# Attention and token mixing on one core: a tile's values in one transfer, and a new table of the order of all work

## The chip, the cores and the metric

The kernel runs on one core of a Trainium2 chip. The core has five instruction streams that matter here: TensorE (PE: matrix products; its weight loads, PEld, overlap them), VectorE (DVE), ScalarE (ACT), GpSimd (POOL) and SyncE (SP, which issues every transfer of this kernel). The metric is the device time of one execution in microseconds (us); lower is better. The text gives medians over several executions, and the profile is one further execution.

## The reference

Two stages follow each other on a batch of 4 sequences of 768 positions (8 heads of 64, so 512 columns); everything is float32.

```python
# attention: each position sees the positions less than 16 away, and 24 block summaries
k_sum = k.reshape(B, H, nb, 32, D).max(axis=3)
v_sum = v.reshape(B, H, nb, 32, D).mean(axis=3)
scores_l = where(|i - j| < 16, scale * q @ k.T, -1e9)
scores_s = scale * q @ k_sum.T + log(32)
a = softmax(concat(scores_l, scores_s))
x = a @ concat(v, v_sum)                       # [4, 768, 512]
# mixing
theta = x @ w_theta
zr, zi = x * cos(theta), x * sin(theta)
y = w_tok_r @ zr + w_tok_i @ zi                # over the 768 positions
u = x + y
out = u + maximum(u @ w_ch, 0)
```

## The kernel before

The work is written as a list of small operations, each with its engine or a choice of engines. A table of numbers, `ORDER`, names every operation once, in the order in which all of them are issued; a letter behind a number picks the engine (g GpSimd, d VectorE, a ScalarE). Each engine takes its own operations in that order, strictly one behind the other, and waits on semaphores for what an operation needs. So the table alone decides what stands ahead of what on each engine. One rule is added at issue: a GpSimd operation that shares the memory port with VectorE waits for the VectorE operation that precedes it in the table.

Attention works in 24 tiles (4 batches of 6) of 128 positions, each in two halves of 64 queries. For a tile (`att_tile`) SP loads q (`q<-qg`, 256 KB, two buffers), the values (`v<-vg`) and, for batches 1 to 3, the keys. TensorE forms the scores (line 523), VectorE subtracts the maximum (559), ScalarE takes the exponential (563), TensorE turns the result (572), ScalarE or VectorE copies it out (578), and TensorE multiplies it with the values (`products`, 546). The values of a half are 96 rows of 2,080 bytes (8 heads of 64 numbers and a one, which sums the weights), 195 KB; 24 rows of block summaries are copied in ahead of them. There are four value buffers, so a tile's values can only land once the products of two tiles before have ended.

Then the tile is turned back (605), and the theta product follows: for the first 6 tiles in plain float32 (639), later as three products of split numbers (644), four groups each into one bank `t`. Rounding, sine and cosine follow (655 to 668, on ScalarE and VectorE), and the product with x (674, half on VectorE, half on GpSimd) gives the input of the token mixing. Batches 0 and 1 are mixed directly (702, `mix_step`, the products M), tile by tile. Batches 2 and 3 use a scheme with seven products MP1 to MP7 (817, `mix_fast`). Each MP has 12 pieces of three matrix products (6 tiles, two column halves). MP6, MP7, MP5 and MP3 take summed weights, streamed by SP from `s_scratch` into the second halves of six `wt` buffers (384 KB each); a buffer is loaded anew when the last piece that reads it has ended. At the end the channel product with `w_ch` (922) and the relu follow, and SP writes the output.

At most 8 transfers are under way: each one waits for the end of the one issued eight before.

Of the kernel before, what the change touches and what calls it, by code (L numbers as in the profile page):

```python
# [29 lines left out]
NK = NB + NL  # L30
VL = 96
# [27 lines left out]
253 104 85 98 215 214 110 223 216 296g 258 224 99d 225 243 255 257 217 118 348g 226 105 227 218 119g 220d 293 256 245 219d 106
244 246 228 247 250 111 120 221 291 121 249 222d 248 123 124g 297 229 122 349g 298 345 259 230 260 262 292 299 261 270 130 125  # L60
301 350g 115 300 271 263 126 272 303 423g 305 302 304 306 273 267d 308 131g 307 116 264d 419 310 135 268 309 265 274 313 127
136g 132 311 312 266d 141 275 269d 314 276 133 315 142g 137 317 316 277 138 352 143 112 231 325 326 318 232 134 327 163 233g
139 144 353 361 168 319d 356 328 320 329 362 278 330 322 355 234 169g 145 331 346 164g 321d 279 364 323 363 282 117 146 324
283 420 332 354 113 347 284 280 365 474 285 147 380 358 114 357 339 165 360 148 366 359 337 166 367 338 149 167 170 368 150
152 381 424 369 422 333 370 400 153 382 128 383 384 171 334 154 172 155 157 281 158g 156 425 385 371 402 401 159 372 386 340
174 335 175g 373 426 392 394 374 421 160 375 377 376 378 387 529 161 404 176 388 379 403 705g 389 454 177 530 179 395 393 178
180 455 456 390g 472 408 457 181 405 182 410 183 427 703 458 459 414 466 409 412 460 461 462 463 411 435 428 467 429 704g 406
437 706g 438 415 431 430 441 468 615g 469 413 436 434 464g 707 521 442 433 465 432 416 417 407 479g 440 564d 523 443 439 480
288g 741 709g 534 444 446d 418 481 535 482 445 485 483 447 490 477 129 492 491 484 475 448 478g 493 486 496 449 451d 532 710g
452 743 450d 488 531g 522 453d 497 616g 487 536 509 537 539 494 586 476d 540 489 538 495 498 510 621 499 391g 501 543 500d 541  # L70
742 511 502 512 545 503 506 513 542 547 551 504 546 733 507 583 289g 286g 708g 549 505d 550 533g 343g 548 544 745 508d 514 744
552 553 515 341 554 555 524 516 556d 517 711 712 518 287g 713d 714 739 585 336g 557 344g 398 734 587 596 558d 599 519 624 588
603 559 715 592 589 716 746 717 561 668 568 591 562 565g 622 735 593 718 566 719 584 560d 597 140 601 720 595 563 598 567 600
602 399g 784 590 594 623 342 569 785d 604 473g 721 786 740 605 572 625 607d 570 634 606 576 608 626 635 787g 617 788 653g 722
618 665 638 151 789 629 574 697 637 630 396d 397g 470 619 525g 723g 737 639 627 790 698g 609d 620 636 628 520 832 612 633 736
471g 162 641 833g 654g 659g 613 738 834g 631 791 640 610 611d 632 792 614d 655 841 642 747 752 643 835g 669 526 644d 793 645
670 646 812 678 672 657 679 650 813d 671 173 667 683 681 658 814d 815 680 663 647d 836 673 748 842 816 675 664 684 843g 817
656 648 818 755 754 724 945g 837 674 682 844 819 660g 677 661 649d 651 666 527d 652 676 685 820 686 687 794 839 689 821 688d
795 838g 756 1015 757 690 528g 571 845g 975 765 662 822 759 760 976d 850 691 840 977d 578 846 978 851g 796 768 823 727d 763
184 797 852 946 699 766 758 692 853g 769 1020 701 694d 979 940 702 980 700 941 847g 772 848 693d 579 981 825 767 695 749 696d  # L80
761 762 771 731 753 750 764 580g 798d 824 982 728 770 732 773 983 774 775d 984 947 956 581g 776 854g 777 995 948 729 778d 959
849 781d 949 950 958 725g 582g 802 952 803 996 997 998 953 799g 859 751 943 1016 1021 779 951 782 855 999 730 780 1074 1000
985 860g 1001 856 800 726 963 1018 808 857 1002 942 954 861g 957 961 960 962 801 955 575 826g 783 964 862 863g 1077 858 944g
965 1003 1022 966 1004 986 967d 864g 968 1005 806 804 1017g 810 1031 972 868 805 865g 1050 828 1023 1051d 1052 1032 869g 573
577 987 829 1170 1053 830 1024 866 1025 1033 989g 1006 969d 1054 827 1035 1037 831 1029 1055 870 1028 993 871 1056 1007g 970
872g 1027 1034 867 973 1120d 1038 1008 877 994 1036 1026 1057 1019d 1058 1013 1030 971 1014 974d 873d 1059 1039 874g 1040 1042
1078 878 1041d 809 811 990g 1079 1043 1047d 1208 1076 807 1087 1089 991 876 992 1209 1088 1090 1011 1210d 1083 1094 1093 1044d
1060 879 1009 880 1211 1080 1212 875 881 1082 1129 1012 1045 882g 1048 1213 886 1061 1126 1081 1092 1066 883 1075 1010 884
1084 1091 1214 1063g 1085 887 1067 885 1062 1127 1121 1046d 988 888 1215 1086 1173 1068 1049 1216 895 1095 1096 1098 1106g
1130 1217 1097d 889 1099 1218d 1279 1107g 1280 1281g 1069 1131 1070 896 1071 1228 1133 1100d 1282 1064g 1219 1135 890 1103d  # L90
1229 1283 1072 1073 1139 1065 891g 1137 1132 1110 1141 892 1142 1101 1284 1111 897 1143 1104 1285 1134 1138 1102d 898g 1108
1105d 1145 899g 1146 1286 1140 1144 1136 1109 1287 1128 893 900d 1158d 1147 1148 901g 1150 894 1288 1172 1250 1149d 1118 1174
1289 1114 1175 1112 1151 1305 1116 1178 1179 902 1202 1236 1122 1152 1183 903 1221g 1123 1306 1124 1185 1307 1308g 1187 1177
1181 1309 1153 904 1182 1160 1184 1232 1310 1155 1189 1237 1230 1233 1220g 1188 1176 1125 1186 1311 905 1156 1162 1171 1290
1312 906g 1249 1154 1163 1203 1247 1190 1180 1157 1234 1313 1159g 1191 1192 1193 1291g 1231 1251 1314 1222g 1194d 907 1315d
1252 1254 1195 1235 1292g 1117 1354 1240 1196 1253 1355 1260 1261 1356 1161 1199d 1255 1357g 1166 1168 1319 1197 1358 1198d
1322 1256 1257 1241 1258 1164d 1165g 1169 908g 1316 1263 1242 1200 913 1359 1206 1264 1360 1259 1207 1201d 1243 909 1324 1361
# [1025 lines left out]
```

## Time and profile before

| | |
|---|---|
| time, median of 3 runs | 435.1 us (434.0 to 435.14) |
| profiled execution, span from the first to the last instruction | 435.6 us |
| TensorE busy | 421.7 us, 97% |
| VectorE busy | 352.2 us, 81% |
| ScalarE busy | 280.3 us, 64% |
| GpSimd busy | 209.7 us, 48% |
| transfers: share of 16 DMA engines' time on the queue | 71.1% |

The profiled execution's span is 0.5 us longer than the median of the runs. The busy shares are means over the span; the start, the mixing of the first tiles and the end have limits of their own.

### The profile page before, as it was taken

To read this page: it belongs to the slowest core of one execution; us is meant where nothing else is said; L and a number is where in the kernel's file an instruction comes from. 1 tells how busy PE (TensorE), PEld (TensorE's weight loads), DVE (VectorE), ACT (ScalarE), POOL (GpSimd) and SP (SyncE) were. 2 spreads that over 40 slices of the span, in tenths; PEclk is the share of its full clock that TensorE was granted. 3 is DMA by queue.
4 is the path that set the end of the run, shared out by engine and by line. 5 is a ranking of instruction groups with operands and counts; after the bars stand their busy time and mean duration, and the time that the engine had idled before them with its cause. 6 is when DMAs were issued, how large, how long until landed. Compare 5 with 4: busy or idle time off the path is not lost.

```text
span 435.6 us, 10044 instructions
## 1 busy us (share of the span) xinstructions
PE 421.7 (97%) x3682; PEld 350.9 (81%) x3682; DVE 352.2 (81%) x947; ACT 280.3 (64%) x600; POOL 209.7 (48%) x208
## 2 busy tenths in 40 slices
PE   5989999998999999999999999999999989999996
PEld 1455555665888888888888899999899989999996
DVE  3799999778988777875757695866489989999996
ACT  1799995787757784866785885493955447455210
POOL 3543324687775665245465578624453410251542
PEclk9899999999999999999999999999999999999999
DMA  8999956989678678848767987883379696220138
GB/s 294 347 354 364 295 197 208 290 257 322 230 233 273 197 224 266 259 139 247 232 188 223 292 273 218 245 246 119 111 230 338 229 367 223 75 73 20 65 136 289
DMA packets 76321, 100.07 MB, mean 230 GB/s; under 512 B 23024, under 2 KB 58864, under 8 KB 76272
## 3 DMA queue, kind: packets, MB, share of 16 engines
q1 hardware_dynamic: 76272, 99.43, 71.1%
q8 instruction: 29, 0.48, 0.5%
q14 instruction: 20, 0.16, 0.1%
HBM read 75.82 MB, written 23.59 MB: 228 GB/s over the span
## 4 chain that ended last, share of the span: by engine, by line
PE 87%; DMA 10%; DVE 1%; ACT 1%; SPq 0%; issue 0%; POOL 0%; DVEq 0%
PE m L702 25%; PE m L817 19%; PE t L644 11%; PE c L922 7%; PE m L922 6%; PE pa L546 5%; PE s L523 4%; PE t L639 3%; PE t L605 3%; DMA q<-qg 3%; PE pa L572 3%; DMA wth<-wth 2%; DMA wt<-wti 2%; DMA zu<-kT 2%; DMA wt<-s_scratch 1%; PE t L922 1%
## 5 line engine op out<-in xcount | busy, mean ns | idle before, releaser
L817 PE MATMUL m<-wt,hl 128*128 128x384 f32 x504 | 95.7, 339 | 1.4 <-DMA wt<-s_scratch 1.2
L817 PEld LDWEIGHTS m<-wt,hl 128*128 128x128 f32 x504 | 87.7, 188 | 4.9 <-ACT hl L309 1.5
L702 PE MATMUL m<-wt,hl 128*128 128x512 f32 (+1 forms) x432 | 84.9, 341 | 0.0
L702 PEld LDWEIGHTS m<-wt,hl 128*128 128x128 f32 x432 | 68.6, 188 | 10.8
L563 ACT ACTIVATE e<-e,st 128x118 f32<-128x118 f32 x192 | 63.1, 388 | 12.1 <-DVE st L559 11.6
L559 DVE CUSTOM_DVE_ANT_0 e<-s,cs 128x118 f32<-128x118 f32 x192 | 46.8, 272 | 9.6 <-PE s L523 4.7
L318 POOL TENSOR_TENSOR hl<-zu,hl 128x512 fp32r<-128x512 f32 x23 | 30.1, 1309 | 43.9 <-DMA wt<-s_scratch 15.9
L644 PE MATMUL t<-wth,xh 128*128 128x512 f32 x144 | 45.3, 396 | 0.0
L674 POOL TENSOR_TENSOR zu<-xn,zu 128x512 f32<-128x512 f32 x20 | 27.0, 1350 | 20.3 <-ACT zu L668 5.5
L657 DVE SCALAR_TENSOR_TENSOR zu<-zu,t 128x512 f32<-128x512 f32 x24 | 16.4, 684 | 24.4 <-ACT zu L655 24.4
L702 PE MATMUL m<-wt,zu 128*128 128x512 f32 (+1 forms) x96 | 33.4, 491 | 1.2 <-DVE zu L674 1.2
L655 ACT ACTIVATE zu<-t,bmagic 128x512 f32<-128x512 f32 x24 | 16.5, 687 | 23.9 <-PE t L644 18.3
L309 ACT CAST hl<-zu 128x512 fp32r<-128x512 f32 x31 | 19.1, 619 | 18.2 <-PE m L817 14.9
L702 PEld LDWEIGHTS m<-wt,zu 128*128 128x128 f32 x96 | 17.5, 190 | 15.8 <-issue 12.6
L546 PEld LDWEIGHTS pa<-v,e 118*64 118x64 f32 x768 | 24.8, 137 | 6.8 <-issue 3.0
L318 DVE TENSOR_TENSOR hl<-zu,hl 128x512 fp32r<-128x512 f32 x37 | 27.6, 751 | 2.3 <-ACT hl L309 2.1
L523 PE MATMUL s<-k,q 64*64 64x118 f32 x768 | 25.6, 272 | 3.9 <-POOL cs L340 3.2
L546 PE MATMUL pa<-v,e 118*64 118x65 f32 x768 | 28.1, 224 | 1.2 <-ACT e L578 1.2
L730 POOL TENSOR_TENSOR zu<-zu 128x512 f32<-128x512 f32 x15 | 21.4, 1432 | 15.0 <-DVE zu L730 4.9
L644 PE MATMUL t<-wth,xl 128*128 128x512 f32 x72 | 28.6, 397 | 0.0
L674 DVE TENSOR_TENSOR zu<-xn,zu 128x512 f32<-128x512 f32 x28 | 24.7, 884 | 4.8 <-ACT zu L668 4.6
L523 PEld LDWEIGHTS s<-k,q 64*64 64x64 f32 x768 | 20.2, 135 | 9.2 <-POOL cs L343 4.0
(181 smaller groups left out, 909.9 us busy)
## 6 DMA issues: line engine op xcount, KB each, us to landing
wt<-s_scratch SPq DMA_DIRECT2D x48, 384.0 KB, 4.4
v<-vg SPq DMA_DIRECT2D x48, 195.0 KB, 5.3
s_scratch<-f SPq DMA_DIRECT2D x24, 384.0 KB, 3.9
k<-kg SPq DMA_DIRECT2D x18, 376.0 KB, 5.5
q<-qg SPq DMA_DIRECT2D x24, 256.0 KB, 6.0
wt<-wtr SPq DMA_DIRECT2D x6, 768.0 KB, 11.0
wt<-wti SPq DMA_DIRECT2D x6, 768.0 KB, 11.4
f<-kT SPq DMA_DIRECT2D x12, 384.0 KB, 4.3
```

What stands on the lines that cost most here:

```text
L309: nc.scalar.copy(dst(), src())
L318: lambda e: V[e].tensor_tensor(dst(), src(), hi().bitcast(F32), op=ALU.subtract), reads, writes, due, port=BOTH)
L523: mm(0.79 * len(pairs) / NP, [lambda p=p, g=g, h=h: nc.tensor.matmul(sc[h].get()[ROW[g], p], q.get()[ROW[h], p, ROW[g]], k.get()[ROW[h], p ...
L546: mm(2 * 0.433 + scores[0] + (0.2 if scores[0] else 0.0), [lambda n=n, g=g, a=a: nc.tensor.matmul(xa[a].get()[ROW[g], n], turned[g].get()[ ...
L559: op({"DVE": 0.205}, lambda eng, n=n: nc.vector.tensor_tensor_reduce(e()[:, n], sc[n % 2].get()[:, 2 * a + n // 2], mask(m), -SCALE, 3.0e3 ...
L563: op({"ACT": 0.288}, lambda eng, n=n: nc.scalar.activation(e()[:, n], e()[:, n], AF.Exp, bias=st.get()[:, n:n + 1], scale=-1.0), [(st, n)] ...
L644: calls = [lambda t=t, xx=xx, k=k, c=c: nc.tensor.matmul(th.get(), xx.get()[:, c], w_th[c].get()[:, k], start=(c == 0 and t == 0), stop=(c ...
L674: op({"DVE": c_dve(DM, "two"), "POOL": c_pool(DM)}, lambda e, z=z, hc=hc: V[e].tensor_tensor(z(), xn[b, i].get().rearrange("p h d -> p (h ...
L702: nc.tensor.matmul(acc[th](), zz, w[:, TT[th]], start=(s == 0 and r == 0 and t == 0 and (th == 0 or c == 0)), stop=(s == NT - 1 and r == 1 ...
L730: lambda e: V[e].tensor_tensor(dst(), x(), y(), op=ALU.add if sign > 0 else ALU.subtract), reads, writes, due, port=BOTH)
L817: calls = [lambda ref=ref, tt=tt, z=z, s=s, j=j, t=t, x=x, k=k, bank=bank, first=first: nc.tensor.matmul(bank[j].get()[:, :HT], z.get()[:, ...
L922: calls = [lambda k=k, t=t, x=x, y=y: nc.tensor.matmul(to.get(), weights[n][x][0]()[:, k, j * P:(j + 1) * P], operands[n].get()[:, y, k], ...
```

## The change

Two things change. First, a tile's values come in one transfer of 96 rows of 4,160 bytes (390 KB) in place of two of 195 KB. The two halves lie side by side in one buffer, and there are two such buffers in place of four smaller ones; the bytes are the same, the number of value transfers falls from 48 to 24. Second, the whole table `ORDER` is another one. By the two tables TensorE has 548 operations before and after, VectorE 755 and 731, ScalarE 497 and 508, GpSimd 204 and 217, SP 288 and 264 (the 24 transfers). What is computed is unchanged. In the changed kernel most line numbers are lower by one.

```diff
 ORDER = """
--17g 8 0g 1g 31 23 27 25 9 24 18 29 10 28 2 26 39 3 19 32 30 20 4 44g 33 5 6g 190g 49g 46 45 48 7 50 86 194g 47 193 51 60 61 34
...
+23 8 25 27 13 9 17g 24 26 15 39 31 43g 29 33 18 85 35 28 19 78 184 40 92 20 45 99 44 47 185 21 49 14 10 32 48 0g 1g 2 3 4 30
...
-            A1=13, T1=10, PREP=5, QB=2, VSPE=1, VB=4, KB=2, STR=2, ...
+            A1=13, T1=10, PREP=5, QB=2, VSPE=1, VB=2, KB=2, STR=2, ...
...
-            vbuf[b] = [Ref(apool, [NB + VL, H, DV], tag="v", bufs=K["VB"]) for _ in range(K["VB"])]
+            vbuf[b] = [Ref(apool, [NB + VL, 2, H, DV], tag="v", bufs=K["VB"]) for _ in range(K["VB"])]
...
-        v = [vbuf[b][(2 * i + g) % K["VB"]] for g in range(2)]
+        v = vbuf[b][i % K["VB"]]
+        dma(lambda: v.get()[NB:], lambda: vg[b, i], 2 * H * (VL + 16) * DV * 4, [], [(v, "loc")], due, 4160, 0.35)
         for g in range(2):
-            dma(lambda g=g: v[g].get()[NB:], lambda g=g: vg[b, 2 * i + g], H * (VL + 16) * DV * 4, [], [(v[g], "loc")], due, 2080, 0.35)
-            if 2 * i + g < K["VB"]:
+            if i < K["VB"]:
                 op({"POOL": ...}, lambda e, g=g: (
-                    nc.scalar.copy if e == "ACT" else V[e].tensor_copy)(v[g].get()[:NB], vs.get()), [vs], [(v[g], "sum")], due, port=BOTH)
+                    nc.scalar.copy if e == "ACT" else V[e].tensor_copy)(v.get()[:NB, g], vs.get()), [vs], [(v, ("sum", g))], due, port=BOTH)
...
-            xa[a].get()[ROW[g], n], turned[g].get()[...], v[g].get()[:NK, NH * a + n], start=True, stop=True)
-            for a in range(2) for n in range(NH) for g in range(2)] + scores[1], v + turned + scores[2], xa + scores[3], due, mode="block")
+            xa[a].get()[ROW[g], n], turned[g].get()[...], v.get()[:NK, g, NH * a + n], start=True, stop=True)
+            for a in range(2) for n in range(NH) for g in range(2)] + scores[1], [v] + turned + scores[2], xa + scores[3], due, mode="block")
```

Three places of the new order follow. The first is SP's queue in the first 40 us. Before, from the third q to the fifth (the fifth q is the one ahead of the last `v` row shown), it reads:

```order
L303 DMA q<-qg 128x512
L303 DMA v<-vg 96x520 x2
L303 DMA wt<-wtr 128x1536
L303 DMA wt<-wti 128x1536
L303 DMA q<-qg 128x512
L303 DMA wt<-wtr 128x1536
L303 DMA v<-vg 96x520 x2
L303 DMA wt<-wti 128x1536
L303 DMA wt<-wtr 128x1536
L303 DMA v<-vg 96x520
L303 DMA q<-qg 128x512
L303 DMA v<-vg 96x520
```

In the changed kernel SP's queue reads, from the second tile's values to the fourth tile's:

```order
L302 DMA v<-vg 96x1040
L302 DMA q<-qg 128x512
L302 DMA wt<-wtr 128x1536
L302 DMA wt<-wti 128x1536
L302 DMA q<-qg 128x512
L302 DMA wt<-wtr 128x1536
L302 DMA v<-vg 96x1040
L302 DMA wt<-wti 128x1536
L302 DMA wt<-wtr 128x1536
L302 DMA q<-qg 128x512
L302 DMA v<-vg 96x1040
```

The fifth q now stands ahead of all of the fourth tile's values, where one half of them preceded it before. It is the 28th transfer before and the 24th after, and the bytes ahead of it fall by that half.

The second place is TensorE at tile 5's first mixing product (`m<-wt,zu`, the first row of that form below; `t<-wth` are the four groups of tile 6's theta product, each of two rows). Before:

```order
L644 MATMUL t<-wth_926,xh 128x512 x2
L644 MATMUL t<-wth_926,xl 128x512
L644 MATMUL t<-wth_887,xh 128x512 x2
L644 MATMUL t<-wth_887,xl 128x512
L644 MATMUL t<-wth_972,xh 128x512 x2
L644 MATMUL t<-wth_972,xl 128x512
L702 MATMUL m_722<-wt,zu 128x512
L702 MATMUL m_704<-wt,zu 128x256
L644 MATMUL t<-wth_1011,xh 128x512 x2
L644 MATMUL t<-wth_1011,xl 128x512
L702 MATMUL m_702<-wt,zu 128x512
L702 MATMUL m_704<-wt,zu 128x256
```

After, the same place on TensorE:

```order
L643 MATMUL t<-wth_689,xh 128x512 x2
L643 MATMUL t<-wth_689,xl 128x512
L643 MATMUL t<-wth_739,xh 128x512 x2
L643 MATMUL t<-wth_739,xl 128x512
L643 MATMUL t<-wth_954,xh 128x512 x2
L643 MATMUL t<-wth_954,xl 128x512
L643 MATMUL t<-wth_912,xh 128x512 x2
L643 MATMUL t<-wth_912,xl 128x512
L701 MATMUL m_718<-wt,zu 128x512
L701 MATMUL m_683<-wt,zu 128x256
L701 MATMUL m_681<-wt,zu 128x512
L701 MATMUL m_683<-wt,zu 128x256
```

The fourth theta group has moved ahead of the first mixing product of tile 5.

The third place is TensorE where batch 3 goes from MP6 to MP7. The number behind `wt` is the weight buffer, that behind `hl` the operand. Before, the last eight pieces of MP6 and the first four of MP7 (the buffers of MP7 in their order: 1206, 1235, 1495, 1498, 1507, 1832):

```order
L817 MATMUL m2_4508<-wt_1495,hl_4579 128x384 x3
L817 MATMUL m0_4556<-wt_1495,hl_4579 128x384 x3
L817 MATMUL m0_4556<-wt_1498,hl_4579 128x384 x3
L817 MATMUL m2_4508<-wt_1498,hl_4579 128x384 x3
L817 MATMUL m2_4508<-wt_1507,hl_4601 128x384 x3
L817 MATMUL m2_4508<-wt_1832,hl_4601 128x384 x3
L817 MATMUL m0_4556<-wt_1507,hl_4601 128x384 x3
L817 MATMUL m0_4556<-wt_1832,hl_4601 128x384 x3
L817 MATMUL m2_4508<-wt_1206,hl_4629 128x384 x3
L817 MATMUL m2_4508<-wt_1235,hl_4629 128x384 x3
L817 MATMUL m0_4556<-wt_1206,hl_4629 128x384 x3
L817 MATMUL m0_4556<-wt_1235,hl_4629 128x384 x3
```

After, the same stretch (the buffers of MP7 in their order: 1012, 1193, 1154, 1553, 1462, 1887):

```order
L816 MATMUL m0_4549<-wt_1154,hl_4582 128x384 x3
L816 MATMUL m0_4549<-wt_1553,hl_4582 128x384 x3
L816 MATMUL m2_4467<-wt_1154,hl_4582 128x384 x3
L816 MATMUL m2_4467<-wt_1553,hl_4582 128x384 x3
L816 MATMUL m2_4467<-wt_1462,hl_4568 128x384 x3
L816 MATMUL m0_4549<-wt_1462,hl_4568 128x384 x3
L816 MATMUL m0_4549<-wt_1887,hl_4568 128x384 x3
L816 MATMUL m2_4467<-wt_1887,hl_4568 128x384 x3
L816 MATMUL m0_4549<-wt_1012,hl_4590 128x384 x3
L816 MATMUL m0_4549<-wt_1193,hl_4590 128x384 x3
L816 MATMUL m0_4549<-wt_1154,hl_4608 128x384 x3
L816 MATMUL m2_4467<-wt_1012,hl_4590 128x384 x3
```

The fifth buffer (1507 before, 1462 after) is now free one piece earlier, and the third (1495 before, 1154 after) is needed earlier: seven pieces lie between the end of its use in MP6 and its first use in MP7, where ten did.

## Rows read from the trace of the kernel before

**Rows 1.** The page, busy time by engine: us, share of span, instructions.

```profile
PE 421.7 (97%) x3682; PEld 350.9 (81%) x3682; DVE 352.2 (81%) x947; ACT 280.3 (64%) x600; POOL 209.7 (48%) x208
```

**Rows 2.** Waits of TensorE: line, releaser, us in total, times, longest.

```profile
PE s L523 <- POOL cs L340: 3.2, 1, 3.2
PE t L379 <- POOL zu L377: 1.4, 1, 1.4
PE m L702 <- DVE zu L674: 1.2, 1, 1.2
PE pa L546 <- ACT e L578: 1.2, 2, 0.7
PE m L817 <- DMA wt<-s_scratch: 1.2, 1, 1.2
PE s L523 <- DMA q<-qg: 0.4, 1, 0.4
PE m L817 <- DVE x L826: 0.2, 1, 0.2
```

**Rows 3.** Windows: us, busy PE, PEld, DVE, ACT, POOL, PEclk, DMA share, GB/s.

```profile
11.00:45.00 34.00, 31.36 (x399) 18.11 (x400) 30.83 (x127) 30.44 (x73) 15.57 (x27) 0.95 1.04 354
364.00:432.00 68.00, 67.81 (x388) 67.32 (x387) 66.57 (x107) 25.47 (x43) 24.12 (x14) 1.00 0.35 121
```

**Rows 4.** Critical chain from 20 to 46 us: start, us, what.

```profile
18.58 9.06 DMA wt<-wti
...
27.66 11.64 DMA q<-qg
...
39.44 1.04 PE s L523 x32
```

**Rows 5.** Windows in which value rows move (first) and don't (second).

```profile
28.00:31.00 3.00, 3.00 (x26) 1.28 (x29) 3.00 (x14) 3.00 (x9) 1.17 (x2) 1.00 1.05 300
24.00:28.00 4.00, 3.34 (x55) 2.48 (x52) 3.96 (x16) 4.00 (x11) 1.32 (x3) 1.00 1.01 405
```

**Rows 6.** Critical chain from 90 to 103 us.

```profile
89.73 2.15 PE t L639 x5
...
97.62 2.31 DVE zu L674
...
99.98 1.56 PE m L702 x4
101.54 0.70 PE t L644 x3
```

**Rows 7.** GpSimd's timeline beside it: start, us, engine, line, operation.

```profile
97.55 1.83 POOL L318 TENSOR_TENSOR wt<-wt 128x768 fp32r<-128x768 f32 x1
```

**Rows 8.** Line 674 on VectorE: duration in ns, min/median/max.

```profile
L674 DVE TENSOR_TENSOR zu<-xn,zu x28: 659/685/2303, 45.1 to 330.5; 128x512 f32<-128x512 f32 x28
```

**Rows 9.** Critical chain from 335 to 360 us.

```profile
345.49 5.85 DMA wt<-s_scratch
...
353.31 0.57 DVE x L826
```

**Rows 10.** TensorE's timeline, pieces of MP1 to MP7 back to back.

```profile
326.02 24.26 PE L817 MATMUL m<-wt,hl 128*128 128x384 f32 x138
```

**Rows 11.** Transfer issued at 341.33, first for MP7: us from issue to landing.

```profile
wt<-s_scratch SPq DMA_DIRECT2D x1, 384.0 KB, 3.5
```

**Rows 12.** Transfer issued at 342.89, third for MP7.

```profile
wt<-s_scratch SPq DMA_DIRECT2D x1, 384.0 KB, 4.6
```

**Rows 13.** Transfer issued at 346.10, sixth for MP7.

```profile
wt<-s_scratch SPq DMA_DIRECT2D x1, 384.0 KB, 6.2
```

**Rows 14.** Transfer issued at 351.36, behind twelve others of that burst.

```profile
wt<-s_scratch SPq DMA_DIRECT2D x1, 384.0 KB, 9.2
```

**Rows 15.** Window of MP7's first load (columns as in rows 3).

```profile
341.00:343.00 2.00, 2.00 (x13) 2.00 (x12) 2.00 (x5) 1.15 (x3) 0.00 (x0) 1.00 0.17 17
```

**Rows 16.** The wait for bank t, from TensorE's timeline.

```profile
32.81 0.66 PE L605 MATMUL t<-cs,xn 128*128 128x128 f32 x4 [0.68 <-DVE zu L657]
```

More of the change, by code (lines that the diff above doesn't have):

```diff
@@ L59 @@
[L59 to L62, printed above, removed]
@@ new lines @@
+180 469 403 400 387 285 429 450 698 451 452 181 453 454 182 404 693g 455 405 695g 406 462 432 463 388 460 522 456 431 457
+458g 286g 421 424 423 409 428 696d 410 425 407 408 556 401 430 461 514 427 435 433 411 434 412 422 426 436 699g 516 437 438
+402 472g 439 440d 283 526 413g 339g 332g 473 474 475 471g 477 476 481 441 527 478 442 483 443 515 445 722 482 479 446 724
+444d 447d 480 284g 502 486 485 487 730 484 488 150 490 723 470g 489 491 725 386g 503 575 577 528 492 494 523 493d 697g 524
+391g 529 504 495 531 535 496 497 537 539 466g 530 541 538 533 337g 525g 532 731 505 506 507 459g 540 499d 536 542 498d 534
@@ new lines @@
+1589 1677 1449 1454 1456 1555 1590g 1666 1669 1672 1667 1670 1680 1594 1675 1673 1556 1683 1475 1439 1514 1515 1516g 1436
+1518 1458 1455 1597d 1448 1450 1452 1437 1557 1702 1438d 1440 1598g 1459 1676 1679 1443 1678 1681 1684 1682 1685 1457 1604g
+1711 1447 1453 1451 1474 1558 1686 1460 1717 1461 1441 1462 1463 1476 1559d 1464d 1600g 1465 1466 1611g 1742 1477 1470 1687
+1689 1688 1601d 1479 1467 1602 1478 1481 1468 1608g 1743 1690 1692 1471 1694 1519 1480 1485 1744g 1691 1606d 1607g 1693 1695
+1696 1697 1560 1745 1699 1616 1746 1747 1517g 1612d 1482 1748 1486 1484 1469d 1472 1613 1489 1749 1483 1490 1487 1491 1520
@@ new lines @@
+1731 1734 1723 1726 1729 1732 1799 1737 1721 1724 1727 1766 1767 1769g 1546 1547 1778 1814g 1768 1815g 1779 1780d 1548 1886
+1784 1730 1889 1785 1786 1806 1787 1733 1736 1739 1735 1738 1898 1895 1807 1800d 1788 1789 1790 1791 1781 1801 1826 1741 1855
+1804g 1805g 1857 1783 1859 1740 1792 1869 1793 1856 1858 1871 1782 1860 1862 1827 1861 1873 1875 1823 1794 1795 1796 1802
+1883 1797 1803 1864 1863 1865 1808d 1809 1877 1892 1867 1866 1822g 1977 1978 1812 1818 1879 1819 1990 1870 1813 1979 1996
+1872 1874 1868 1997 1831 1998g 1820 1876 1991 1878 2020 2022 1840 1881 1816g 1880 1882 1830 1992g 1824 2021 1817 1843 1884
@@ new lines @@
+2050 2064d 2066 2095 2067 2053 2166 2054 2093 2057 2060 2154 2164 2098 2073 2070 2061 2074 2155 2077 2078 2071 2108 2081
+2096g 2187 2111 2217 2209 2075 2079 2102 2058 2218 2132 2128 2134 2107 2113 2100 2112 2082 2076 2109 2224 2150g 2103 2129
+2120 2151 2110 2121 2116 2130 2105g 2114 2156 2133 2117 2141 2152 2131 2135 2137 2142 2153g 2124 2138 2118 2139 2188 2167
+2143 2226 2161 2171 2145 2122 2157 2192 2159 2160g 2072 2125 2115 2162 2158g 2146 2247 2083 2189 2190 2168 2173 2194 2165
+2163 2210 2193 2169 2211g 2191 2136 2170d 2172 2055 2197 2201 2212 2198 2199 2213g 2200 2176 2180 2221 2205 2177 2195 2248
@@ L141 @@
+2219 2080 2126 2174 2175 2184 2202 2144 2178 2220g 2214 2196 2254 2185 2206 2215 2228 2255 2059 2227d 2181 2147 2229 2216
+2222g 2249 2233 2140 2119 2186 2230 2234 2203 2062 2250 2182 2236 2235 2256 2252 2251 2253 2051 2223 2231 2179 2232d 2183
+2237 2257 2258 2261 2225g 2207 2259 2260 2123 2240 2262 2238 2204 2239 2241 2242 2244 2245 2243 2246 2263 2264 2265 2266 2267
 """
@@ L546, in products @@
         mm(2 * 0.433 + scores[0] + (0.2 if scores[0] else 0.0), [lambda n=n, g=g, a=a: nc.tensor.matmul(
-            xa[a].get()[ROW[g], n], turned[g].get()[:NK, (NH * a + n) * QT:(NH * a + n + 1) * QT], v[g].get()[:NK, NH * a + n], start=True, stop=True)
-            for a in range(2) for n in range(NH) for g in range(2)] + scores[1], v + turned + scores[2], xa + scores[3], due, mode="block")
+            xa[a].get()[ROW[g], n], turned[g].get()[:NK, (NH * a + n) * QT:(NH * a + n + 1) * QT], v.get()[:NK, g, NH * a + n], start=True, stop=True)
+            for a in range(2) for n in range(NH) for g in range(2)] + scores[1], [v] + turned + scores[2], xa + scores[3], due, mode="block")
         for a in range(2):
```

147 lines of the change are left out of this document (63 added, 84 removed).

## The prediction

> **What bounds the kernel now.** I read the page first: TensorE is busy 97% of the span, VectorE 81%, GpSimd under half [rows 1]. The matrix products are the same before and after, so TensorE's idle time is all that a new order can win: 435.6 - 421.7 = 13.9 us, of which its waits make some 9.5 us [rows 2]; the remaining 4 us, the first loads and the output after the last product, can't be had. The second view is TensorE's list of waits, which says where the rest lies [rows 2]: 4.6 us in two waits of the first 11 us, 2.3 us in the start-up of attention (the copies of line 578, bank t at line 605, the fifth q) [rows 2, 16], and two single holes of 1.2 us, one at the first mixing product of tile 5, one in the streamed weights of batch 3. Everything else is 0.2 us. The third view, the windows, tells two stages apart [rows 3]: from 11 to 45 us the DMA engines are full (share 1.04, 354 GB/s) while TensorE has 2.6 us of idle time; from 364 to 432 us TensorE is busy 67.81 of 68 us with VectorE at 66.57. The last stage has nothing to win, the middle one the two holes. The chain that ended last shows what the start waits for [rows 4]: not a value transfer and not an engine, but a weight transfer of 9.06 us, whose end lets SP issue the fifth q, which takes 11.64 us to land; TensorE starts on it at once.
>
> **The change, part by part.** All sums are made against the profile's 435.6 us, 0.5 us above the median of 435.1.
>
> The merged values by themselves. No wait of TensorE or of the chain names the values [rows 2, 4]. A product needed both halves before and needs them now; a buffer comes free after the same product. SP issues 24 transfers fewer, but nothing in the chain waits for SP's own issuing time. I put 0 on it directly. It has one indirect effect, on the start: while rows of 2,080 bytes move, the queue carries 300 GB/s, otherwise 405 [rows 5]. By the time the fifth q is needed three tiles' values (3 x 390 KB = 1.17 MB) have moved; at 300 GB/s that is 3.9 us, at 405 it is 2.9. The new rows of 4,160 bytes may get any part of this, 0 to 1.0 us; I take 0.4, since the first window is a mix of values and weights, so that the values alone are slower than its mean, and doubling the row will not make them as fast as rows of 6 KB.
>
> The fifth q. It is TensorE's release at 39.44. In the new order one half of the fourth tile's values (195 KB) no longer moves ahead of it, the rest ahead is the same bytes: 195 KB / 354 GB/s = 0.55 us [rows 3]. With the 0.4 us above q lands about 0.95 us sooner. To profit, TensorE must be there sooner: it came 0.44 us early before [rows 2], and the new order takes the copy of the first tile out from behind an operation that waits for a transfer, and issues the first keys ahead of the block values; the waits at line 578 (1.2 us) are what this can shorten. I take **-0.9 us**, from -0.3 (only the half transfer, q sharing the full queue) to -1.5. After 39.44 TensorE has no further wait for a transfer until 350, so this shift is kept.
>
> Tile 5's first mixing product. The hole: tile 5's theta ends at 89.73 + 2.15 = 91.88, its product with x at 97.62 + 2.31 = 99.93, 8.05 us later; TensorE goes on at 99.98, 8.1 us after 91.88, and 1.2 us of this is the wait, so that its other work covers 6.9 us [rows 2, 6]. The new order puts the fourth theta group (0.70, rows 6) ahead too: 7.6 us of cover. What makes the chain long is VectorE's operation at 97.62: 2.31 us, where the median of its kind is 0.685 [rows 6, 8]. It started 0.07 us after a GpSimd subtraction of 1.83 us and ended 0.55 us after that one's end [rows 7], as if it had run only then. In the new order that GpSimd subtraction (another weight piece by then) stands just ahead of the product with x on VectorE, and no longer behind a product with x of another tile on GpSimd, so that it can start sooner and overlap only in part. If the block goes, the chain is 8.05 - 1.62 = 6.4 us, below 7.6: the hole goes altogether, -1.2. If it stays whole, 8.05 - 7.6 = 0.5 us remain, so -0.7. I take **-1.1**.
>
> The Trainium skill, page "SBUF — State Buffer", section "SBUF: two separate sides", has a rule for this: VectorE with two SBUF inputs and GpSimd reading SBUF share one port pair as an exclusive lock, and whichever starts second waits for the whole other instruction. The 2.31 us beside the GpSimd operation's 1.83 agree with it. By the rule alone, with GpSimd's subtraction starting first again, the term is -0.7; by the row's median it is -1.2.
>
> MP7 of batch 3. A piece takes 24.26/46 = 0.527 us [rows 10]. Before, nine pieces (4.74 us) lie between the release of the fifth buffer and its next use; its load took 5.85 us [rows 9], so TensorE waited 5.85 - 4.74 = 1.1, shown as 1.2 [rows 2]. Now ten pieces (5.27 us) lie there, for the first, fourth and sixth too, nine for the second, but seven (3.69 us) for the third. The third load took 4.6 us [rows 12]; it would be late by 0.9, or by 0 if it lands as the first did, in 3.5 [rows 11]; I take 0.4. The sixth took 6.2 us [rows 13] against 5.27 plus those 0.4: 0.5 late. So 0.8 to 0.9 us of waiting in place of 1.2: **-0.3 us**, between -1.2 (all land in time) and +1.0 (the third takes 5.85: 2.2 late).
>
> Banks. Between two MP groups VectorE adds the bank to the output (0.57 us, rows 9) before the next group may write to it. One piece of 0.52 us covered it once before, and cost 0.2 us [rows 2]; by the new order one piece must do three times (MP1 to MP6, MP6 to MP7, MP7 to MP4), one of them swallowed by the weights' wait: **+0.3**, 0 to +0.6.
>
> New tight places. Between a theta product and the next user of bank t, by the order and the products' durations, TensorE has 1.57 us of other work at the tiles X1 and X2 and 1.64 at X20; one of the three waited, 0.68 us [rows 16]. By the new order X1 and X2 keep 1.57, X10 and X22 have 1.65, X20 is relieved. One more such place at a third of 0.68 is +0.2; I double it for places of other kinds (the turned weights straight ahead of the first value product, scores of tile 1 with 2.7 us before their turn where there were 4.7): **+0.4**, 0 to +1.5.
>
> VectorE in the last stage loses some 3 us of work to ScalarE and GpSimd there, but TensorE waited 0.19 us of 68 [rows 3]: 0. If VectorE's cover of 1.4 us is misplaced by a new local order, that could cost the same 1.4; I leave it in the range.
>
> Sum: -0.9 - 1.1 - 0.3 + 0.3 + 0.4 = -1.6 us: 434.0 for a profile, 435.1 - 1.6 = **433.5** for the median. The likeliest case's own range is 432 to 434.3.
>
> **The rivals.** (a) *The gains go back; no change.* At the start the queue is full whatever its order, and with eight transfers under way a value transfer of 390 KB in place of 195 takes a larger share of it: if two of the eight ahead of q are such, 390 KB more at 354 GB/s are 1.1 us, and q lands 0.55 us later instead of earlier. Then +0.5 stands for -0.9, and -1.1 - 0.3 + 0.3 + 0.4 with it gives -0.2: 434.9. For it: the 11.64 us of the q, more than its own bytes need by ten times, say that it shares [rows 4]. Against: the bytes ahead are fewer. It takes in the case that the merging does nothing and VectorE stays blocked: -0.55 - 0.7 - 0.3 + 0.3 + 0.4 = -0.9, 434.2.
>
> (b) *Slower: the third streamed weight.* With 3.69 us of cover the third buffer of MP7 is the most exposed place of the new order. On an empty queue loads land in 3.5 to 4.6 us, on a loaded one in up to 9.2 [rows 11, 12, 14]. Seven other transfers (channel weights, the stored u) are issued just ahead; before, the queue was nearly empty (share 0.17) when MP7's first load was issued [rows 15]. They hang on the last theta product of the program, which the new order puts about 1 us later; if they still move, the load takes as long as in the burst: 9.2 - 3.69 = 5.5 us late in place of 1.2. With the other terms, -0.9 - 1.1 + 0.3 + 0.4 + 4.3 = +3.0: 438.1. It decides above a landing of 7.5 us: there the term is +2.6 and the total +1.3, the edge of what can be measured. Against: 1 us later leaves a part of the 2 us of empty queue.
>
> (c) *The holes go and nothing new comes*: -0.9 - 1.2 - 1.2 = -3.3, 431.8. Against: the order is tight everywhere; each wait that it has comes from a coincidence of two engines, and a new order draws these again.
>
> **How the numbers follow.** About 1.3 us (0.3%) is what can be told from no change here; faster means under 433.8, slower over 436.4. The forecast (a gain of 0.8 to 3) has 0.5, (c) 0.1, (a) 0.22, (b) and other new waits of its kind together 0.18. Of the forecast's half a quarter lies within 0.3%, since its centre is only 0.3 us beyond the edge. So: faster 0.47 (0.37 of the forecast, 0.1 of (c)), same 0.35, slower 0.18. The range reaches from (c) with a margin, 431.2, to 436.4, and leaves out the upper part of (b).
>
> **What would show it.** The fifth scores product at 38.3 to 39.0 instead of 39.44, with q still the last wait or none: right. The first mixing product of tile 5 without a wait, the VectorE product with x near 0.7 us: right; at 2.3 us again with half a microsecond of wait: it stayed blocked. At MP7 of batch 3 a wait under 1 us at the third or sixth buffer: right; several us at the third: (b). Values in the chain or in TensorE's waits, or a TensorE idle of several us in the stage after 364, would make the whole account wrong.

## The result: slower by 1.0%

The changed kernel takes 439.6 us (median of 6 runs, 437.7 to 441.4), the kernel before beside it 435.1 (6 runs, 434.0 to 435.7): a ratio of 1.0102, with a 95% interval from 1.0075 to 1.0129. The forecast was 433.5, the range 431.2 to 436.4.

First a correction to the base of the sum. In each run of both kernels the time is some 1.75 us longer than the span. The profile of before (span 435.6) thus belongs to an execution of about 437.4 us, and not to one that is half a microsecond off the median. A second profile of the same kernel (before_again, below) has a span of 433.6 and a time of 435.3. It is the better base, and stands for before from here on.

The page of the changed kernel, busy time by engine (as in [rows 1]):

```profile
PE 424.0 (97%) x3682; PEld 351.3 (80%) x3682; DVE 348.4 (79%) x923; ACT 291.9 (67%) x627; POOL 214.4 (49%) x221
```

TensorE's waits in the changed kernel (as in [rows 2]), the ones that matter here:

```profile
PE s L522 <- DMA q<-qg: 2.1, 2, 1.4
PE t L378 <- POOL zu L376: 1.8, 1, 1.8
PE pa L545 <- ACT e L577: 1.7, 3, 0.9
PE pa L571 <- ACT e L562: 1.5, 1, 1.5
...
PE m L816 <- DMA wt<-s_scratch: 0.5, 1, 0.5
...
PE m L816 <- issue: 0.3, 1, 0.3
...
PE m L701 <- POOL zu L673: 0.3, 1, 0.3
PE m L816 <- DVE x L825: 0.2, 1, 0.2
```

The wait of 1.2 us at tile 5 is gone, that of the streamed weights is under 1 us. New are two waits in the start: 1.4 us for the second tile's q (the longer of the two in the first row), and 1.5 us for ScalarE's exponentials of tile 1, which is the second tile. Windows of the changed kernel (columns as in rows 3):

```profile
11.00:45.00 34.00, 29.47 (x378) 17.66 (x379) 28.67 (x115) 29.64 (x72) 12.56 (x22) 0.95 1.03 320
20.00:24.00 4.00, 2.44 (x36) 1.54 (x36) 2.32 (x17) 3.24 (x11) 2.27 (x4) 1.00 1.02 258
36.00:40.00 4.00, 4.00 (x23) 1.75 (x20) 4.00 (x17) 4.00 (x13) 2.71 (x2) 1.00 1.06 230
23.80:27.50 3.70, 3.67 (x52) 2.72 (x52) 3.17 (x6) 3.70 (x9) 0.36 (x2) 0.71 1.01 405
```

The queue is as full as before (share 1.03) but carries 320 GB/s where it carried 354 [rows 3]; 230 to 258 while values move. The last row shows TensorE's clock behind the idle time of 1.48 us: 0.71, a mixture of its two levels (2.4 and 1.2 GHz). TensorE's timeline there, and at the scores product that had waited for the fifth q:

```profile
23.76 1.30 PE L571 MATMUL pa<-cs,e 64*118 64x64 f32 x16 [1.48 <-ACT e L562]
24.99 0.83 PE L604 MATMUL t<-cs,xn 128*128 128x128 f32 x4
25.76 1.85 PE L522 MATMUL s<-k,q 64*64 64x118 f32 x32
...
40.39 1.04 PE L522 MATMUL s<-k,q 64*64 64x118 f32 x32
...
47.11 1.13 PE L701 MATMUL m<-wt,zu 128*128 128x512 f32 x2
```

At half the clock 32 scores products take 1.85 us, else 1.04. The scores product starts at 40.39, against 39.44 [rows 4] and 38.47 in the second profile. It no longer waits there, but q has landed only just before: issued at 27.70, it took

```profile
q<-qg SPq DMA_DIRECT2D x1, 256.0 KB, 12.6
```

so it landed at 40.3, against 39.30 [rows 4] and 38.3 in the second profile.

Where the 4.9 us between the two spans arise is seen if TensorE's start of a product is set against the sum of the median durations of the products before it. That difference is its lateness. Worked out from the traces (us), after so many us of work:

```
work done            36     63     84    320    end
before_again       16.1   16.8   19.4   23.2   24.6
changed kernel     18.5   21.3   22.9   27.5   29.6
v_one              17.7   19.4   22.5   29.0   29.7
v_late             17.0   17.6   20.3   24.1   26.7
swap2              17.3   19.7   20.8   25.3   27.0
one_warm           18.4   19.9   20.9   25.4   27.1
z5_late            16.4   17.0   18.2   21.7   22.6
```

36 us of work lies behind the start of the first mixing product (44.70 us in before_again, 47.11 in the changed kernel: 2.4 us apart there too), 84 behind tile 5's, 320 ahead of the waits in MP7. The changed kernel loses 2.4 us up to the first mixing product, another 2.1 by 63, wins 1.0 back at tile 5, loses 0.8 in the 236 us that follow, and 0.7 in MP7 and behind. Each row is one execution. The two executions of before lie 1.0 us apart at the first mixing product (45.65 and 44.70) and 2.0 at the end, and v_late's took 2.1 us more than the median of its kernel; so a single difference under some 2 us in this table shows a place, and is no proof of a cost.

The 2.1 us hang on a chain that begins in the start. The chain of the changed kernel in the window from 46 us on, thinned out:

```profile
34.22 17.42 DMA wt<-wti
...
51.73 0.91 ACT f L400
...
53.14 0.95 DVE f L408
...
58.27 4.31 DMA f<-kT
...
75.97 2.51 POOL wth L317 x2
...
79.36 1.31 POOL zu L673
...
80.72 1.56 PE m L701 x4
```

A raw weight lands at 51.64; its conversion to float32 on ScalarE and VectorE, and the transfers and engines that wait for it, are then the chain for 29 us. In the second profile of before the chain from 40 to 84 us consists of TensorE's own products and nothing else. That the late start is the whole cause isn't shown: swap2 (below) starts its mixing 1.2 us sooner than the changed kernel and still loses 1.7 us against before_again in this stretch (17.3 to 19.7, against 16.1 to 16.8).

At the streamed weights the chain that ended last reads (as in [rows 9]):

```profile
346.37 4.53 DMA wt<-s_scratch
...
356.01 0.57 DVE x L825
```

It is the load of the third buffer, the third of MP7's six, and took 4.5 us; before, the chain went through the fifth buffer's, which took 5.85.

### The profile page after: what moved, and what is told of

Same layout as the page of the kernel before. It is cut to its first block, busy times and chain, and to the rows that moved or that the text cites. A ratio compares the mean times of both kernels' runs of the same rounds, so it can differ in the third digit from the quotient of the medians.

```text
span 438.5 us, 10014 instructions
## 1 busy us (share of the span) xinstructions
PE 424.0 (97%) x3682; PEld 351.3 (80%) x3682; DVE 348.4 (79%) x923; ACT 291.9 (67%) x627; POOL 214.4 (49%) x221
## 4 chain that ended last, share of the span: by engine, by line
PE 77%; DMA 14%; DVE 5%; ACT 2%; issue 1%; POOL 1%; SPq 0%; ACTq 0%; DVEq 0%; POOLq 0%
PE m L701 20%; PE m L816 18%; PE t L643 11%; PE c L921 6%; PE m L921 5%; PE pa L545 5%; PE s L522 4%; DMA wt<-wti 4%; DMA v<-vg 3%; PE pa L571 3%; PE t L604 2%; DMA q<-qg 2%; DMA f<-kT 2%; DMA zu<-kT 1%; DVE wt L411 1%; DMA wt<-s_scratch 1%
## 5 line engine op out<-in xcount | busy, mean ns | idle before, releaser
L816 PE MATMUL m<-wt,hl 128*128 128x384 f32 x504 | 92.9, 339 | 1.1 <-DMA wt<-s_scratch 0.5
L816 PEld LDWEIGHTS m<-wt,hl 128*128 128x128 f32 x504 | 87.1, 188 | 3.5 <-issue 2.3
L701 PE MATMUL m<-wt,hl 128*128 128x512 f32 (+1 forms) x432 | 80.5, 340 | 0.0
L701 PEld LDWEIGHTS m<-wt,hl 128*128 128x128 f32 x432 | 67.0, 188 | 10.0
L317 POOL TENSOR_TENSOR hl<-zu,hl 128x512 fp32r<-128x512 f32 x28 | 38.4, 1374 | 47.3 <-DVE cb L729 8.2
L308 ACT CAST hl<-zu 128x512 fp32r<-128x512 f32 x34 | 21.0, 620 | 29.2 <-PE m L816 18.4
L673 POOL TENSOR_TENSOR zu<-xn,zu 128x512 f32<-128x512 f32 x23 | 30.8, 1341 | 15.6 <-ACT zu L667 13.9
L643 PEld LDWEIGHTS t<-wth,xh 128*128 128x128 f32 x144 | 25.5, 188 | 5.1
L729 POOL TENSOR_TENSOR f<-f 128x192 f32<-128x192 f32 x35 | 21.6, 620 | 14.6 <-DVE st L588 5.1
L577 ACT COPY e<-pa 118x512 f32<-118x512 f32 x32 | 18.2, 590 | 11.5 <-PE pa L571 11.5
L317 DVE TENSOR_TENSOR hl<-zu,hl 128x512 fp32r<-128x512 f32 x32 | 23.7, 742 | 1.9 <-POOL hl L310 1.7
```

Source lines behind the costliest of these rows:

```text
L308: nc.scalar.copy(dst(), src())
L317: lambda e: V[e].tensor_tensor(dst(), src(), hi().bitcast(F32), op=ALU.subtract), reads, writes, due, port=BOTH)
L643: calls = [lambda t=t, xx=xx, k=k, c=c: nc.tensor.matmul(th.get(), xx.get()[:, c], w_th[c].get()[:, k], start=(c == 0 and t == 0), stop=(c ...
L673: op({"DVE": c_dve(DM, "two"), "POOL": c_pool(DM)}, lambda e, z=z, hc=hc: V[e].tensor_tensor(z(), xn[b, i].get().rearrange("p h d -> p (h ...
L701: nc.tensor.matmul(acc[th](), zz, w[:, TT[th]], start=(s == 0 and r == 0 and t == 0 and (th == 0 or c == 0)), stop=(s == NT - 1 and r == 1 ...
L729: lambda e: V[e].tensor_tensor(dst(), x(), y(), op=ALU.add if sign > 0 else ALU.subtract), reads, writes, due, port=BOTH)
```

## The experiments

The first four runs cross the kernel before with the changed one. Each run is timed against the kernel before on its own chip; the numbers are the median in us, its ratio to before and the 95% interval.

**v_one**: before's table; a tile's values in one transfer, at the place of the first half.

```diff
-v (half), q, v (half)
+v (whole tile), q
```

> The order of before, with a tile's values in one transfer, put where the first half's transfer stood; nothing else differs from before. Theory A (the loss comes from the new order, the single transfer costs nothing by itself): 435.1, between 434.4 and 435.8. Theory B (a transfer of 390 KB holds up the other transfers of the full queue at the start and so the whole kernel): 437 to 439.5.

440.3 us, ratio 1.0111 [1.0073, 1.0149]. The merging at this place costs as much as the whole change does.

**v_two**: the changed table, each transfer of values split in two, one behind the other.

```diff
-v<-vg 96x1040
+v<-vg 96x520 x2
```

> The order of the changed kernel, with a tile's values in two transfers again, one straight behind the other. Theory A: no better than the changed kernel, 438.5 to 440.5. Theory B: most of the loss is gone, 435 to 437.

438.5, 1.0073 [1.0045, 1.0102]. The new table alone costs too. That it costs less than with one transfer isn't told apart: the intervals overlap.

**start_before** and **start_after**: one transfer; the two tables put together at the first mixing product, start_before with before's start and the changed remainder, start_after with the changed start and before's remainder.

> The changed kernel (one transfer), with the order of before for all operations that stand ahead of the first mixing product, the new order behind it. Theory A, with the loss mainly in the start (first mixing product 1.46 us later, TensorE at half clock from 23.8 to 29 us): 436.5 to 438, the first mixing product near 45.7. Rival: the loss lies mainly between the first mixing product and 93 us (1.66 us of new waits): 438.5 or more.

> The reverse: the new order up to the first mixing product, the order of before behind it, one transfer. Theory A, loss mainly in the start: 436.5 to 438, first mixing product near 47.1. Rival (the loss lies behind the start): 435 to 436.

437.8, 1.0063 [1.0031, 1.0094], and 443.6, 1.019 [1.014, 1.0241]. With before's start in front the changed remainder does not cost more than before's (v_one, 440.3, whose interval overlaps). The latter run, slower than either theory had it, has a wait of 2.9 us for ScalarE at a theta product, which v_one and the changed kernel don't have. The seam between the two tables can make such a wait, so this run gives no price for the changed start.

**before_again**: no edit.

> The kernel before, profiled a second time; nothing is changed. Its shown profile has a span of 435.6 us, while the medians belong to spans of about 433.4 (the time is some 1.75 us longer than the span in every run). Theory 1: the two single holes of 1.2 us, at tile 5's first mixing product and at MP7 of batch 3, are of that one execution; then this profile has a span near 433.4, and one or both are under 0.4 us. Theory 2: they are there in every execution; then they are 1.0 to 1.4 us again, and the 2 us lie in the start.

435.3, span 433.6. TensorE's waits:

```profile
PE s L523 <- POOL cs L340: 1.6, 1, 1.6
...
PE m L702 <- DVE zu L674: 1.2, 1, 1.2
...
PE m L817 <- DMA wt<-s_scratch: 0.2, 1, 0.2
```

The hole at tile 5 is there both times; that of MP7 (1.2 in [rows 2]) and half of the first wait are not.

**v_rows** and **v_pad**: v_one with other rows in DRAM (the first diff is v_rows, the second v_pad).

```diff
 v_rows: one transfer of 192 rows of 2,080 bytes
-vg[b, i]
+vg[b, i].rearrange("g p h d -> p g h d")
 v_pad: rows of 4,160 bytes that begin 4,352 apart
+np.pad(..., ((0, 0), (0, 0), (0, 0), (0, 48)))
```

> The kernel before's order and the changed kernel's two buffers and 24 value transfers of 390 KB (as in v_one, 440.3), but the source keeps its two halves apart, so that one transfer is 192 rows of 2,080 bytes in place of 96 of 4,160. Theory 1 (the length of the row slows the queue): back to 435.0 to 436.5, and the windows in which values move carry some 300 GB/s, as before. Theory 2 (the size of the transfer or the two big buffers cost the time, whatever the row): 439.0 to 441, as v_one.

> As v_one (the kernel before's order, one transfer of 96 rows of 4,160 bytes), but the rows in DRAM lie 4,352 bytes apart, so that each begins on a multiple of 256 bytes. Theory 1 (rows of this length are slow wherever they begin): 439.5 to 441, as v_one, 215 ns for a row. Theory 2 (it is the place where a row begins): 436 to 438, a row near twice the 85 ns of a row of 2,080 bytes.

439.3, 1.008 [1.0052, 1.0108], and 442.0, 1.0141 [1.0098, 1.0183]. With short rows in one transfer the loss stays, and long ones that begin on a multiple of 256 bytes don't help. The length of the row, my first theory, is not the cause.

**w3_later**: the changed kernel, the four operations that turn and split one weight piece put behind tile 1's exponentials.

```diff
-W3 (four operations), SM of tile 1
+SM of tile 1, W3 (four operations)
```

> The changed kernel, with the four operations that turn and split the first theta weight's fourth piece put behind the last exponential of tile 1, so that ScalarE no longer waits for that weight ahead of the exponentials. Theory 1 (this wait delays the start and with it all that follows): the 1.48 us of idle time ahead of tile 1's turned weights falls under 0.5 us, the clock stays full there, the first mixing product comes 0.8 us or more sooner than 47.1, and the time is 438.2 to 438.9. Theory 2 (what comes later is late through other transfers, and takes the gain): the start is sooner but the time stays 439.2 to 440.

438.9, 1.0094 [1.0057, 1.0132]: not told apart from the changed kernel. The idle time of 1.48 us shrinks to 0.63, but the theta product then waits 1.24 us for the piece that was put off, and the first mixing product starts at 47.09, as in the changed kernel (47.11). This theory fell.

**v_late** and **v_adj**: v_late is v_one with the transfer at the place of the second half; v_adj has before's 48 transfers and four buffers, the second half moved up behind the first.

```diff
 v_late, fourth tile
-v<-vg 96x1040, q<-qg 128x512
+q<-qg 128x512, v<-vg 96x1040
 v_adj, fourth tile
-v<-vg 96x520, q<-qg 128x512, v<-vg 96x520
+v<-vg 96x520 x2, q<-qg 128x512
```

> The kernel before's order, a tile's values in one transfer as in v_one (440.3), but the transfer stands at the place of the second half in SP's queue, where v_one has it at that of the first; so the fifth q again has no byte more ahead of it than before, and fewer by 195 KB. Theory 1 (the merging costs by its place: half a transfer more ahead of the fifth q and its like): the fifth scores product starts at 38.9 or sooner, TensorE's clock stays full at 30 to 45 us, time 435 to 437. Theory 2 (390 KB of value rows in a row slow the queue wherever they stand): TensorE waits about 1 us for the third tile's values or the fifth q again, time 438.5 to 440.5.

> The kernel before with its 48 value transfers of 195 KB and four buffers; only the second half of a tile is moved up in SP's queue, directly behind the first. So the bytes stand in v_one's order, without any merging. Theory 1 (the place of the bytes costs the time, not the merging): 438.5 to 440.5, as v_one and v_rows. Theory 2 (one transfer of 390 KB costs it, by being counted as one of eight under way or by taking all DMA engines at once for longer): 435 to 436.5.

435.2, 1.0002 [0.9982, 1.0023], and 438.9, 1.0088 [1.0063, 1.0112]. This is the decisive pair: merged at the second half's place the values cost nothing that can be told, and unmerged at the first half's place they cost as much as in v_one. In before's table it is the place of the bytes in the queue. Both edits move the bytes of every tile; which tile's cost how much was not run. In v_adj the fifth q lands at 38.8, half a microsecond behind the 38.3 of before_again, as 195 KB at 354 GB/s would have it (in before's first profile it landed at 39.30, so this is within what executions differ by). What v_adj's profiled execution makes of it is seen in TensorE's timeline and the window behind it:

```profile
38.97 1.04 PE L523 MATMUL s<-k,q 64*64 64x118 f32 x32 [1.78 <-DMA q<-qg]
40.00:44.00 4.00, 4.00 (x40) 2.96 (x39) 4.00 (x15) 3.24 (x5) 0.04 (x1) 0.57 1.04 348
```

In before_again the same product waited 0.88 us, and the same window has the full clock:

```profile
38.47 1.04 PE L523 MATMUL s<-k,q 64*64 64x118 f32 x32 [0.88 <-DMA q<-qg]
40.00:44.00 4.00, 4.00 (x40) 2.45 (x40) 4.00 (x14) 3.89 (x7) 0.64 (x1) 1.00 1.06 379
```

TensorE came there 0.4 us sooner than in before_again and q 0.5 later, so the wait is 0.9 longer. Then the way from this product to the first mixing product, 6.2 us in before_again (38.47 to 44.70), takes 7.7 (38.97 to 46.68) at the lower clock. That makes 2.0 of the 3.3 us between the two spans by there; the rest is lost behind 63 us of work. In v_one TensorE's wait is another one, 1.0 us for the third tile's values (window from 32 to 36 us at 0.71). v_late's profiled execution took 437.3 us: it too waits for the third tile's values, 1.00 us, with a granted clock of 0.57 in that window, and its scores product starts at 39.42, not at the 38.9 expected.

**sb_two** and **m05_two**: two transfers, before's table up to the first mixing product, or up to tile 5's theta product; the changed table behind it.

> Two transfers for a tile, the kernel before's order up to the first mixing product (some 46 us), the changed kernel's order behind it. The same with one transfer took 437.75. Theory 1 (the new order's start costs 2 us or more, and what stands behind it gives 1.2 back at tile 5 and loses as much at 48 to 75 us): 434.5 to 436. Theory 2 (the new order behind the start costs by itself, since it was worked out for other lateness): 437 or more.

> Two transfers for a tile, the kernel before's order up to tile 5's theta product (some 90 us), the changed kernel's order behind it. Theory 1 (the wait of 1.2 us at tile 5's first mixing product is in every execution of before, and the new order there removes it without a new wait): 433.6 to 434.4, better than both kernels. Theory 2 (the new order later on, at 100 to 330 us, gives it back in small waits): 435 to 436.

436.2, 1.0016 [0.9996, 1.0036], and 443.4, 1.018 [1.0157, 1.0203]. With before's start the changed remainder costs nothing that can be told, and v_two, the same remainder behind the changed start, lies 2.3 us above it with an interval that doesn't overlap. So the changed start costs some 2 us, without any merging. By its lateness sb_two is 1.2 us ahead of before_again behind tile 5 (18.2 at 84 us of work), and 1.0 behind at the end (25.6). The second run says nothing of tile 5: TensorE waits 5.1 us at the seam for a VectorE operation that the two tables order differently.

Then two edits of the changed kernel's start, and tile 5's wait by itself.

**swap2**: SP's queue of the changed kernel, two pairs exchanged, as before has them.

```diff
-v<-vg 96x1040
 wth<-wth 128x1024
+v<-vg 96x1040
 wth<-wth 128x1024
-v<-vg 96x1040
 q<-qg 128x512
+v<-vg 96x1040
```

> The changed kernel (439.6); in SP's queue only the first tile's values change places with the theta weight behind them, and the second tile's values with the third q behind them, as the kernel before has them. Theory 1 (value rows that move early and beside q's rows slow the queue in the new order's start): 11 to 24 us carry 370 GB/s or more, where the changed kernel's windows had 341, 307 and 258; the scores product that follows the fifth q starts 1 us or more sooner than 40.39, and the time is 437 to 438.5. Theory 2 (the places don't matter, the engines' order does): within 0.7 us of the changed kernel.

438.1, 1.0055 [1.0024, 1.0087]. The windows from 12 to 24 us carry 407, 301 and 289 GB/s, the stretch

```profile
11.00:45.00 34.00, 28.98 (x382) 16.76 (x382) 30.14 (x120) 30.93 (x75) 13.12 (x23) 1.00 1.03 337
...
39.36 1.04 PE L522 MATMUL s<-k,q 64*64 64x118 f32 x32 [0.42 <-DMA q<-qg]
```

is at 337 in place of 320, the scores product 1.0 us sooner, and the first mixing product 1.2 (45.87). So by the traces the place of two tiles' values is half of the start's loss; the medians lie 1.5 us apart, but the interval overlaps the changed kernel's.

**one_warm**: the changed kernel with one more useless product ahead of tile 1's turned weights.

```diff
-WARM=5
+WARM=6
```

> The changed kernel with one more useless product on TensorE in its idle time at 22 us, so that the idle time ahead of tile 1's turned weights is shorter than 1.48 us. Theory 1 (the half clock from 24 to 28 us costs the start about 1 us): the granted clock stays full there, the first mixing product comes about 1 us sooner than 47.1, time 438.3 to 439. Theory 2 (the queue sets the end of the start, the fifth q landing at 40.3 whatever TensorE does): the clock may stay full, but the scores product then waits for q, and the time is 439.2 to 440.

438.4, 1.0071 [1.0047, 1.0095]. The idle time goes and the window from 24 to 28 us has the full clock (1.00), but the scores product then waits 0.18 us for the fifth q, at 40.11, and the first mixing product starts at 46.98 in place of 47.11. So the fifth q, and with it the queue, sets the end of this start. The total moved by 1.2 us, which the intervals don't tell from none.

**z5_free** and **z5_late**: before, and v_late, with one GpSimd subtraction of a weight piece put behind tile 5's first product with x.

```diff
-W2 (weight 7, second part) g
 Z (tile 5, first half)
+W2 (weight 7, second part) g
```

> The kernel before (two transfers); one GpSimd subtraction of a weight piece is put behind tile 5's first product with x in the table, so that VectorE is not beside it; nothing else moves. Theory 1 (the blocked VectorE operation is the whole of that wait, as predicted): the operation takes 0.7 us in place of 2.3, the wait of 1.2 us at tile 5's first mixing product goes, 433.8 to 434.3. Theory 2 (the weight piece is then late, or VectorE blocks elsewhere): 435 to 436.

> As z5_free, but with a tile's values in one transfer at the second half's place (v_late, 435.2). If merging at that place is free, and the wait goes: 433.8 to 434.3, better than both kernels. If merging costs something that v_late's interval of 0.2% hides, 434.5 to 435.2.

434.2, 0.9958 [0.994, 0.9977], and 433.4, 0.9944 [0.9923, 0.9965]: both faster than both kernels. TensorE's wait of 1.2 us at tile 5 is in neither profile. The VectorE product and GpSimd's row in z5_free (in before the product took 2.31 us, beside GpSimd's 1.83 [rows 6, 7]):

```profile
97.54 0.69 DVE L674 TENSOR_TENSOR zu<-xn,zu 128x512 f32<-128x512 f32 x1
98.37 1.83 POOL L318 TENSOR_TENSOR wt<-wt 128x768 fp32r<-128x768 f32 x1 [0.86 <-DVE zu L674]
```

## Why the prediction was wrong, step by step

**Merged values: 0.** Right where the transfer stands as in v_late; the term lacked the place. With every second half moved up behind its first, the fourth tile's ahead of a q that TensorE waits for, the same bytes cost 3.7 us unmerged (v_adj) and 5.1 merged (v_one), whose intervals overlap.

**The indirect gain of 0.4, from longer rows.** Wrong: short rows in one transfer cost the same as long ones at that place (v_rows, v_one), and long rows at v_late's place won no time. That value rows slow the queue [rows 5] is right, but not because they are short. Packets of the traces (one is one row's move) that started within 2 us of the time named, with their mean ns:

```
from                 values      beside them
14 us, v_late         19 x 166   128 of 4,096 B x 165; 107 of q x 86
20 us, changed        56 x 335    68 of q x 152
34 us, v_late         53 x 309    30 of 6,144 B x 451
38 us, changed        31 x 386    36 of 6,144 B x 512
42 us, changed         none      137 of 6,144 B x 238
```

A row of 4,160 bytes takes from 166 to 386 ns, and the rows beside it are slowed about as much. How many of them move does not decide it: v_late at 18 us has 59 at 207 ns, the changed kernel at 38 us 31 at 386. Why isn't shown.

**The fifth q: -0.9.** This is the step that failed. The sum "the rest ahead is the same bytes: 195 KB / 354 GB/s" took the rate for a constant of the queue. The bytes were fewer as said, but the queue carried 320 GB/s, and q landed at 40.3 instead of sooner. v_late, with the same transfers ahead of the fifth q in another order, has its q at 38.0 and 361 GB/s from 11 to 45 us:

```profile
11.00:45.00 34.00, 30.81 (x368) 17.79 (x368) 30.50 (x125) 29.81 (x69) 14.19 (x23) 0.95 1.03 361
```

So in place of -0.9 the start gave +2.4 us to the first mixing product against the second profile, and +1.5 against the first. By the traces half of this is the place of the first two tiles' values (swap2, whose q lands at 39.3). The other half, some 1.2 us, I have not taken apart: the order of the engines' work and the rest of the queue's order are both left. The sum also took the shift for kept, with nothing behind it: in fact 2.1 us more were lost by 63 us of work, in the chain that begins with the raw weight that landed at 51.64.

**Tile 5: -1.1.** Right: -1.0 by the lateness, and no wait at the product. The cause is shown by z5_free, where the operation takes 0.69 us and the whole 1.2 us go. In the changed kernel the VectorE operation still takes 1.27 us there:

```profile
101.50 1.27 DVE L673 TENSOR_TENSOR zu<-xn,zu 128x512 f32<-128x512 f32 x1 [0.23 <-ACT zu L667]
```

GpSimd's subtraction began 1.14 us ahead of it, took 1.87, and ended 0.54 us ahead of its end. That agrees with the Trainium skill's rule (page "SBUF — State Buffer", section "SBUF: two separate sides") that of the two engines the one that starts second is blocked until the other's instruction ends.

**MP7 of batch 3: -0.3.** The waits after are 0.3 and 0.5 us, together the 0.8 to 0.9 of the working, in part by luck. The 0.5 is the third buffer's, forecast at 0.4; the sixth, forecast at 0.5, is not waited for, and the 0.3 has no releaser in the profile. The base was luck too: with before's order there, the wait for these weights is 1.2 and 0.2 us in the two profiles of before, 1.4 in v_late, 0.5 or less in the other seven, while the 0.3 us is in all eight profiles that have the changed order there. So against a typical run the term is a small loss and not a gain. Rival (b), its third buffer 5.5 us late, did not happen.

**Banks: +0.3.** There is one wait of 0.2 us, as in before: 0.

**New tight places: +0.4.** The lateness grows by 0.8 between 84 and 320 us of work, against the second profile; this is less than two executions of one kernel differ by.

Against the second profile: 2.4 + 2.1 - 1.0 + 0.8 + 0.7 = 5.0 us, where the spans differ by 4.9. Rival (a) had the sign right, a fifth q that lands 0.55 us later; it landed 2.0 us later than in the second profile (1.0 later than in the first). Its reason, the larger share that a transfer of 390 KB takes, is not borne out: v_late has the same transfers and loses nothing.

## What to carry to other kernels

The rate of this full queue was no constant: it changed with which transfers moved at the same time (188 to 425 GB/s in stretches of 2 us of the changed kernel's start), so bytes ahead of a transfer divided by a mean rate tell its landing only while their neighbours stay the same. When transfers are merged, ask whose landing the extra bytes now precede: the half that had stood behind an awaited transfer can cost more than its own time, since TensorE's longer wait was followed by half the clock (v_adj). Take a second profile of the kernel before, and keep only those holes that are in both: one operation moved at such a hole made the kernel 0.4% faster, where the new order of all of them made it slower.

## What the runs showed of the hardware

- Transfers of this queue landed in the order of their issue through the first 60 us (both kernels, v_one, v_late, v_adj, swap2), so that bytes moved up delay those that they pass: the fifth q landed at 38.0 us in v_late and 39.9 in v_one.
- In a queue whose share was full throughout, value rows and the rows beside them took up to twice their time and more (166 to 386 ns for 4,160 bytes, 238 to 512 for 6,144).
- After an idle time of TensorE of 1.78 us (v_adj) the granted clock was 0.57 in the next window, after 0.88 us (before_again) 1.00. After about 1 us both occurred: the window from 32 to 36 us has 0.57 in v_late (first row) behind 1.00 us, and 1.00 in z5_late (second row) behind 1.14.

```profile
32.00:36.00 4.00, 3.57 (x34) 2.62 (x35) 2.21 (x14) 3.07 (x9) 1.14 (x2) 0.57 1.05 314
32.00:36.00 4.00, 3.44 (x38) 2.21 (x39) 2.83 (x15) 3.71 (x11) 1.14 (x2) 1.00 1.07 338
```
